# Five matmuls of the identity ahead of the third unit's sums of values

## The chip, the core and the metric

The kernel runs on one core of a Trainium2 chip. The metric is the device time of one execution in microseconds (us). Before the change it is 379.29 us, the median of three runs.

## What is computed

Chunked attention with a left and right context and eight memory keys, followed by a gated MLP with a product over the sequence:

```python
# attention: B, H, S, D = 4, 8, 768, 64; chunks of 32, context 16 left and 8 right, 8 memory rows
scores = scale * np.matmul(q_c, k_full.transpose(0, 1, 3, 2))
scores = scores - np.max(scores, axis=-1, keepdims=True)
a = np.exp(scores)
a = a / (np.sum(a, axis=-1, keepdims=True) + 1e-09)
out[:, :, c_start:c_end] = np.matmul(a, v_full)
# MLP: x is the attention's output, (4, 768, 512); d_ff = 1024
h = np.maximum(x @ w_in, 0.0)
u, v = (h[..., :d_ff // 2], h[..., d_ff // 2:])
v_n = (v - mu) / np.sqrt(var + 1e-06)          # mean and variance over the last axis
v_s = np.einsum('ts,bsd->btd', w_spatial, v_n) + b_spatial[None, :, None]
return ((u * v_s) @ w_out).astype(np.float32)
```

## The kernel before

Attention goes by units of four chunks (128 tokens of one batch, all eight heads); there are 24 units, counted from 0. For unit i a step of the loop over `attend` does the following. ScalarE copies the keys into a padded tile (`kmain`, line 394). TensorE (PE) runs a burst of 64 matmuls of 64 columns that make the scores of unit i (`"s"`), and a burst of 64 that make the sums of values of unit i - 1 (`"a"`); both write the one PSUM tile `sx`, in `burst`, and all of them are recorded at line 409. VectorE takes the maximum (line 466), subtracts it (line 470), ScalarE exponentiates (line 475), VectorE sums and inverts (lines 480 to 483) and multiplies the finished sums of values (line 449). PE transposes the probabilities of unit i (`pt`, line 497) and the finished result of unit i - 1 (`xt`, line 513), and ScalarE and VectorE copy them out of PSUM (lines 500, 518, 522). For units 1 to 5 the two bursts are separate steps of the plan, `"a"` and `"s"`; later they are one.

Between these steps PE runs the first product of the MLP in groups of three matmuls for each quarter of the inner dimension (lines 551 to 553, tile `f`), as soon as the parts of `w_in` and the transposed result are there; ScalarE applies the relu (lines 575 and 612). After the attention come the product over the sequence and the last product (line 700).

The order of all instructions on all engines is written out by `Plan`: each step has an engine, an estimated time, the tiles that it reads and writes, and a rank, and `order` puts the steps in the order of a small simulation. Where this simulation leaves PE idle between 9 and 36 us, `order` puts in spare matmuls of the identity (`busy`, line 249: the 128 x 128 identity as weights, two copies of it as 256 columns to stream, into a PSUM tile `idle` that nothing reads). Loads and stores go through SyncE's queue (SP) in that same order, and `held_by` makes a transfer wait until an earlier one has landed. The values of unit i are loaded by `load_v` in four transfers (into `vmain`); the first matmul of an `"a"` burst waits for these, for the copied probabilities and for the memory rows of the values.

In `burst`, `what` is `"a"` or `"s"` for these units; the step whose `i` is 3 and whose `what` is `"a"` makes the sums of values of unit 2, the third unit.

Of the kernel before, what the change touches and what calls it, by code (L numbers as in the profile page):

```python
# [25 lines left out]
class Plan:  # L26
# [14 lines left out]
    def op(self, eng, us, fn, r=(), w=(), rank=0.0, mb=0.0, tail=0.0, after=None, alone=False, drag=1.0, shared=False):  # L41
        n = len(self.ops)
        deps, begun = set(), set()
        if after is not None:
            begun.add(after)
        for key in r:
            deps.add(self.writer.get(key))
            self.readers.setdefault(key, []).append(n)
        for key in w:
            deps.add(self.writer.get(key))  # L50
            deps.update(self.readers.get(key, ()))
            self.writer[key], self.readers[key] = n, []
        deps -= {None, n}
        held = {k[:2] for k in (*r, *w) if isinstance(k, tuple) and k[0] in self.rings}
        for s in held:
            if s not in self.slots and s[0] not in self.loose:
                if s[0] in self.newest:
                    begun.add(self.newest[s[0]])
                self.newest[s[0]] = n
            self.slots.setdefault(s, []).append(n)  # L60
        begun -= deps
        self.ops.append((eng, us, fn, deps, rank, mb, tail, held, begun, alone, drag, shared))
        return n
# [92 lines left out]
def tile_chunked_attention_gmlp(  # L156
# [47 lines left out]
    op = plan.op  # L204
# [4 lines left out]
    def dve(n):  # L209
        return 0.17 + 0.00102 * n  # L210
# [35 lines left out]
    def busy(k):  # L246

        for _ in range(k):
            nc.tensor.matmul(idle, ident, ident.unsqueeze(1).broadcast_to([P, 2, P]), start=True, stop=True)
# [22 lines left out]
    def wait_for(ins, names, why):  # L272
        for name in names:
            tc.add_manual_dep(ins.ins, name, mybir.DependencyInfo(mybir.DependencyClass.Sync, mybir.DependencyReason.DATA),
                              reason=why)
# [23 lines left out]
    def alloc(name, i, shape, dtype, psum=False):  # L299
        pools = ps if psum else sb  # L300
        a = pools[name].tile(shape, dtype, tag=name, name=name)
        t_[name, i] = a
        return a
# [31 lines left out]
    def qk_keys(i, names="qk"):  # L335
        g, both = i // 2, [0, 1] if i == 1 else [0]
        return [(n, g) + (u, *p) for n in names for u in both for p in ((), ("pad",))]

    def q_of(i):
        return t_["q", i // 2][:, :, (i % 2) * UT:(i % 2) * UT + UT]  # L340
# [4 lines left out]
    def v_of(i):  # L345
        o = (i % NV) * UC
        return vmain[:, :, o:o + UC]
# [24 lines left out]
    def v_keys(i):  # L372
        return [("vm", i, r, s) for r in range(2) for s in range(4)] + \
            [("vmem", i % NV, r) for r in range(2)]
# [29 lines left out]
    def burst(i, rank, split=False):  # L404

        first = []

        def mm(o, w_, m):
            ins = nc.tensor.matmul(o, w_, m, start=True, stop=True, skip_group_check=True)  # L409
            if first:  # L410
                wait_for(ins, first.pop(), "values")

        def go(what):
            if ("sx", i) not in t_:
                alloc("sx", i, [P, 2, 2, T, D], F32, psum=True)
            sx = t_["sx", i]
            if "a" in what:
                first.append([*made["pT", i - 1], *made["v", i - 1], *made["vmem", (i - 1) % NV][-2:]])
            tiles = [(t, c, r, slice(r * D, (r + 1) * D)) for t in range(T) for c in range(UC) for r in range(2)]
            if "s" in what:  # L420
                tq = q_of(i)
                kT = kmain[i % NK].rearrange("p t c s -> p t (c s)")
                for t, c, r, rows in tiles:
                    mm(sx[c * CH:(c + 1) * CH, r, 0, t], tq[rows, t, c * CH:(c + 1) * CH],
                       kT[rows, t, c * SLOT:c * SLOT + WIN])
            if "a" in what:
                pT, vt = t_["pT", i - 1], v_of(i - 1)
                for t, c, r, rows in tiles:
                    mm(sx[c * CH:(c + 1) * CH, r, 1, t], pT[rows, t, c * CH:(c + 1) * CH], vt[rows, t, c])
        whole = ("a" if i >= 1 else "") + ("s" if i < NU else "")  # L430
        for what in (whole if split else [whole]):
            reads, writes = [], []
            us = 0.35
            if "s" in what:
                reads += qk_keys(i, "q") + [("kmain", i % NK), ("kmem", i % NK)]
                writes.append(("sx", i, 0))
                us += 0.5
            if "a" in what:
                reads += [("pT", i - 1)] + v_keys(i - 1)
                writes.append(("sx", i, 1))  # L440
                us += 0.75 if "s" in what else 0.5
            op("PE", us, lambda what=what: go(what), r=reads, w=writes, rank=rank, tail=0.25)
        if i >= 1:
            j = i - 1

            def norm():
                xs = alloc("xs", j, [P, T, 2, D], F32)
                rec = t_["rec", j]
                nc.vector.tensor_tensor(xs.rearrange("p t r d -> p r t d"), t_["sx", i][:, :, 1],  # L449
                                        rec.rearrange("p t r -> p r t").unsqueeze(3).broadcast_to([P, 2, T, D]),  # L450
                                        op=ALU.mult)
            op("DVE", dve(512), norm, r=[("sx", i, 1), ("rec", j)], w=[("xs", j)], rank=rank - 0.5)
        if i < NU:
            softmax(i, rank)

    def softmax(i, rank):
        c0 = (i % UB) * UC

        def top():
            s = t_["sx", i][:, :, 0]  # L460
            if c0 == 0:
                nc.vector.memset(s[0:CH, :, :, 0:LEFT], NEG)
            if c0 + UC == NC:
                nc.vector.memset(s[P - CH:P, :, :, WIN - M:WIN], NEG)
            mx = t_["mx", i] = small.tile([P, 2, T], F32, tag="mx", name="mx")
            nc.vector.tensor_reduce(mx, s, axis=AX.X, op=ALU.max)

        def sub():
            p = alloc("p", i, [P, T, 2, WIN], F32)
            nc.vector.tensor_tensor(p.rearrange("p t r w -> p r t w"), t_["sx", i][:, :, 0],  # L470
                                    t_["mx", i].unsqueeze(3).broadcast_to([P, 2, T, WIN]), op=ALU.subtract)

        def exp():
            p3 = t_["p", i].rearrange("p t r w -> p (t r w)")
            nc.scalar.activation(p3, p3, AF.Exp, scale=scale)

        def den():
            p3 = t_["p", i].rearrange("p t r w -> p (t r) w")
            d = small.tile([P, T * 2], F32, tag="den", name="den")
            nc.vector.tensor_reduce(d, p3, axis=AX.X, op=ALU.add)  # L480
            nc.vector.tensor_tensor(d, d, eps[:, 0:2 * T], op=ALU.add)
            rec = t_["rec", i] = small.tile([P, T, 2], F32, tag="rec", name="rec")
            nc.vector.reciprocal(rec.rearrange("p t r -> p (t r)"), d)

        op("DVE", dve(512) + (0.17 if c0 in (0, NC - UC) else 0), top, r=[("sx", i, 0)],
           w=[("sx", i, 0), ("mx", i)], rank=rank)
        op("DVE", dve(512), sub, r=[("sx", i, 0), ("mx", i)], w=[("p", i)], rank=rank)
        op("ACT", act(512), exp, w=[("p", i)], rank=rank)
        op("DVE", dve(512) + 0.43, den, r=[("p", i)], w=[("rec", i)], rank=rank + 0.6, shared=True)
# [39 lines left out]
    def attend(i, rank, split=False):  # L529
        if i < NU:  # L530
            prep(i, rank)
        burst(i, rank, split)
        flip(i, rank)
# [468 lines left out]
    for b in range(B + 1):  # L1002
        if b < B:
            rank = 300.0 + 10 * b
# [67 lines left out]
```

## Time and profile before

| | |
|---|---|
| median of 3 runs | 379.29 us (375.91 to 380.45) |
| span of the profiled execution | 379.2 us |
| TensorE busy | 357.9 us, 94% |
| VectorE busy | 286.1 us, 75% |
| ScalarE busy | 188.1 us, 50% |
| GpSimd busy | 159.7 us, 42% |

Engines: PE is TensorE's matmuls, PEld its weight loads, DVE VectorE, ACT ScalarE, POOL GpSimd, SP SyncE. Times in the rows are counted from the span's start. A busy share is a mean over stages with different limits; what a change in one stage is worth shows in that stage. In a timeline the bracket at a row's end is the idle time of the engine ahead of it and what ended it; "issue" means that nothing the profile shows ended it. Matmuls are pipelined, so the distance between two starts says more than the time of one. PEclk is TensorE's granted clock: 1.00 is 2.4 GHz, 0.50 is 1.2 GHz.

### The profile page before, as it was taken

To read this page: it belongs to the slowest core of one execution; us is meant where nothing else is said; L and a number is where in the kernel's file an instruction comes from. 1 tells how busy PE (TensorE), PEld (TensorE's weight loads), DVE (VectorE), ACT (ScalarE), POOL (GpSimd) and SP (SyncE) were. 2 spreads that over 40 slices of the span, in tenths; PEclk is the share of its full clock that TensorE was granted. 3 is DMA by queue.
4 is the path that set the end of the run, shared out by engine and by line. 5 is a ranking of instruction groups with operands and counts; after the bars stand their busy time and mean duration, and the time that the engine had idled before them with its cause. 6 is when DMAs were issued, how large, how long until landed. Compare 5 with 4: busy or idle time off the path is not lost.

```text
span 379.2 us, 11840 instructions
## 1 busy us (share of the span) xinstructions
PE 357.9 (94%) x4988; PEld 328.0 (86%) x4988; DVE 286.1 (75%) x479; ACT 188.1 (50%) x334; POOL 159.7 (42%) x155
## 2 busy tenths in 40 slices
PE   2988999999989989989999999999999999999995
PEld 2766787898968968969889898999999999999995
DVE  3878875857747657747389489999979996898893
ACT  3756544555635445434473356346533742653271
POOL 6434562383574086411023275863155124207410
PEclk9998999999999999999999999999999999999999
DMA  8999998788775873876553638404730572140015
GB/s 232 275 194 217 229 271 224 207 257 250 226 218 145 275 214 90 281 206 209 165 206 119 201 124 285 162 3 129 248 124 3 163 246 91 55 155 2 0 45 164
DMA packets 47556, 65.51 MB, mean 173 GB/s; under 512 B 4496, under 2 KB 38928, under 8 KB 47504
## 3 DMA queue, kind: packets, MB, share of 16 engines
q1 hardware_dynamic: 46848, 64.44, 57.3%
q8 instruction: 39, 0.64, 0.7%
q10 hardware_dynamic: 656, 0.33, 0.3%
q14 instruction: 13, 0.11, 0.1%
HBM read 45.88 MB, written 18.87 MB: 171 GB/s over the span
## 4 chain that ended last, share of the span: by engine, by line
PE 82%; DMA 7%; DVE 5%; issue 2%; ACT 1%; SPq 1%; ACTq 0%; DVEq 0%
PE y L700 21%; PE f L700 14%; PE f L551 12%; PE f L552 11%; PE f L553 11%; PE sx L409 8%; DMA vmain<-in_v_dram 6%; PE xt L513 3%; PE pt L497 3%; DVE op L680 2%; DMA big<-in_moe_w_in_dram 2%; DVE sm L663 1%; SPq L278 1%; DVE wout L887 1%; ACT op L677 0%
## 5 line engine op out<-in xcount | busy, mean ns | idle before, releaser
L700 PE MATMUL y<-wsp,op 128*128 128x384 f32 x288 | 52.0, 336 | 0.9 <-ACT st L740 0.9
L754 POOL TENSOR_TENSOR ug<-st,ug 128x384 f32<-128x384 f32 x24 | 36.0, 1515 | 38.5 <-DVE st L746 34.5
L700 PEld LDWEIGHTS y<-wsp,op 128*128 128x128 f32 x288 | 49.9, 188 | 1.2 <-ACT st L740 1.2
L551 PE MATMUL f<-x,win_h 128*128 128x384 f32 x128 | 46.3, 362 | 0.0
L552 PE MATMUL f<-x,win_l 128*128 128x384 f32 x128 | 43.2, 338 | 0.0
L553 PE MATMUL f<-x,win_h 128*128 128x384 f32 x128 | 43.2, 337 | 0.0
L551 PE MATMUL f<-win_h,x 128*128 128x512 f32 x96 | 41.2, 429 | 0.0
L552 PE MATMUL f<-win_h,x 128*128 128x512 f32 x96 | 38.3, 399 | 1.2 <-issue 1.2
L700 PE MATMUL f<-wsp,op 128*128 128x384 f32 x216 | 39.4, 336 | 0.0
L553 PE MATMUL f<-win_l,x 128*128 128x512 f32 x96 | 38.1, 397 | 0.0
L700 PEld LDWEIGHTS f<-wsp,op 128*128 128x128 f32 x216 | 37.6, 188 | 0.0
L680 DVE TENSOR_TENSOR op<-sm,op 128x768 fp32r<-128x768 f32 x32 | 34.8, 1094 | 3.1 <-ACT op L677 2.6
L449 DVE TENSOR_TENSOR xs<-sx,rec 128x512 f32<-128x512 f32 x24 | 16.5, 687 | 27.0 <-PE sx L409 26.9
L587 POOL TENSOR_TENSOR rstd<-ve,mhalf 128x1 f32<-128x1 f32 x24 | 14.6, 608 | 52.0 <-DVE ve L583 49.7
L700 PE MATMUL y<-wout,op 128*128 128x256 f32 x288 | 36.0, 281 | 0.4 <-DVE op L680 0.4
L700 PEld LDWEIGHTS y<-wout,op 128*128 128x128 f32 x288 | 34.8, 188 | 0.9 <-DVE op L680 0.8
L760 POOL TENSOR_TENSOR st<-st,bias 128x384 f32<-128x384 f32 x14 | 18.6, 1337 | 37.2 <-ACT st L740 28.4
L677 ACT CAST op<-sm 128x768 fp32r<-128x768 f32 x32 | 26.2, 837 | 11.6 <-DVE sm L663 10.2
L409 PEld LDWEIGHTS sx<-kmain,q 64*32 64x32 f32 x1536 | 17.0, 107 | 13.9 <-issue 12.0
L388 POOL COPY vmain<-memv 8x1024 f32<-8x1024 f32 x22 | 23.5, 1073 | 11.9 <-PE sx L409 9.8
L409 PE MATMUL sx<-vmain,pT 64*32 64x64 f32 x1536 | 21.9, 226 | 6.1 <-DMA vmain<-in_v_dram 4.1
L409 PE MATMUL sx<-kmain,q 64*32 64x64 f32 x1536 | 20.9, 228 | 6.9 <-ACT kmain L394 6.9
(86 smaller groups left out, 766.3 us busy)
## 6 DMA issues: line engine op xcount, KB each, us to landing
vmain<-in_v_dram SPq DMA_DIRECT2D x48, 128.0 KB
vn_far<-st SPq DMA_DIRECT2D x24, 256.0 KB
u_far<-uo SPq DMA_DIRECT2D x32, 192.0 KB
vr<-vn_far SPq DMA_DIRECT2D x8, 768.0 KB
ug<-u_far SPq DMA_DIRECT2D x16, 384.0 KB
q<-in_q_dram SPq DMA_DIRECT2D x11, 512.0 KB
vmain<-in_v_dram SPq DMA_DIRECT2D x47, 96.0 KB
out_dram<-ot SPq DMA_DIRECT2D x33, 128.0 KB
```

What stands on the lines that cost most here:

```text
L388: ins = {"DVE": nc.vector, "POOL": nc.gpsimd}[eng].tensor_copy(to, of)
L409: ins = nc.tensor.matmul(o, w_, m, start=True, stop=True, skip_group_check=True)
L449: nc.vector.tensor_tensor(xs.rearrange("p t r d -> p r t d"), t_["sx", i][:, :, 1], rec.rearrange("p t r -> p r t").unsqueeze(3).broadcast ...
L551: nc.tensor.matmul(o, lh, rh, start=(j == 0), stop=False)
L552: nc.tensor.matmul(o, ll, rh, start=False, stop=False)
L553: nc.tensor.matmul(o, lh, rl, start=False, stop=(j == len(pairs) - 1))
L587: nc.gpsimd.tensor_tensor(a, t_["ve", i], mhalf, op=ALU.pow)
L677: nc.scalar.copy(half(0), of())
L680: nc.vector.tensor_tensor(half(1), of(), half(0).bitcast(F32), op=ALU.subtract)
L700: nc.tensor.matmul(o, x, y, start=first and m == 1, stop=m == 3 * chunks, skip_group_check=True)
L754: nc.gpsimd.tensor_tensor(g, t_[st(x)], g, op=ALU.mult)
L760: {"DVE": nc.vector, "POOL": nc.gpsimd}[eng].tensor_tensor(a, a, bias[:, 1], op=ALU.add)
```

## The change

The step that makes the third unit's sums of values first calls `busy(5)`: five pairs of weight load and matmul of the identity stand on PE directly in front of the burst's first matmul. The step's estimated time, its reads, writes and rank stay as they were.

```diff
@@ -439,7 +439,11 @@
                 reads += [("pT", i - 1)] + v_keys(i - 1)
                 writes.append(("sx", i, 1))
                 us += 0.75 if "s" in what else 0.5
-            op("PE", us, lambda what=what: go(what), r=reads, w=writes, rank=rank, tail=0.25)
+            def start(what=what):
+                if i == 3 and what == "a":
+                    busy(5)
+                go(what)
+            op("PE", us, start, r=reads, w=writes, rank=rank, tail=0.25)
         if i >= 1:
             j = i - 1
```

## Rows read from the trace of the kernel before

**Rows 1.** The page, engines: busy time, share of the span, instructions.
```profile
PE 357.9 (94%) x4988; PEld 328.0 (86%) x4988; DVE 286.1 (75%) x479; ACT 188.1 (50%) x334; POOL 159.7 (42%) x155
```

**Rows 2.** The chain of waits, 0 to 34 us: start, length, what.
```profile
25.86 7.26 DMA vmain<-in_v_dram
33.12 0.24 issue
```

**Rows 3.** Timeline of PE, 8 to 44 us: start, length, instruction, idle time before.
```profile
8.02 2.67 PE L249 MATMUL idle<-ident 128*128 128x256 f32 x6
...
11.90 5.78 PE L249 MATMUL idle<-ident 128*128 128x256 f32 x26
...
28.23 0.85 PE L409 MATMUL sx<-vmain,pT 64*32 64x64 f32 x64 [1.22 <-DMA vmain<-in_v_dram]
...
29.50 0.60 PE L249 MATMUL idle<-ident 128*128 128x256 f32 x2
...
30.88 0.66 PE L513 MATMUL xt<-ident,xs 128*128 128x128 f32 x4
33.36 0.93 PE L409 MATMUL sx<-vmain,pT 64*32 64x64 f32 x64 [1.83 <-DMA vmain<-in_v_dram]
34.22 0.79 PE L551 MATMUL f<-win_h,x 128*128 128x512 f32 x1
...
36.95 0.92 PE L513 MATMUL xt<-ident,xs 128*128 128x128 f32 x4
37.63 0.48 PE L551 MATMUL f<-win_h,x 128*128 128x512 f32 x1
...
40.47 0.66 PE L497 MATMUL pt<-ident,p 128*128 128x128 f32 x4 [0.36 <-ACT p L475]
40.88 0.48 PE L551 MATMUL f<-win_h,x 128*128 128x512 f32 x1
...
42.45 0.86 PE L409 MATMUL sx<-vmain,pT 64*32 64x64 f32 x64
43.24 0.50 PE L551 MATMUL f<-win_h,x 128*128 128x512 f32 x1
```

**Rows 4.** Stretches: length, each engine's busy time (instructions), PEclk, DMA share, GB/s.
```profile
28.00:31.54 3.54, 3.31 (x138) 2.52 (x138) 2.55 (x7) 2.25 (x5) 2.10 (x3) 1.00 1.04 170
31.54:33.36 1.82, 0.00 (x0) 0.03 (x1) 1.45 (x3) 1.34 (x3) 0.33 (x2) 1.00 0.86 268
34.22:36.95 2.73, 2.73 (x13) 2.04 (x8) 2.56 (x5) 2.07 (x4) 1.00 (x2) 0.50 0.92 194
```

**Rows 5.** Timeline of ScalarE, 37 to 41 us.
```profile
37.91 0.59 ACT L518 CAST x<-xt 128x512 fp32r<-128x512 f32 x1
39.30 0.60 ACT L575 ACTIVATE st<-f 128x512 f32<-128x512 f32 x1 [0.80 <-PE f L553]
39.80 0.62 ACT L475 ACTIVATE p<-p 128x512 f32<-128x512 f32 x1
```

**Rows 6.** Timeline of VectorE, 38 us.
```profile
38.05 0.68 DVE L470 TENSOR_TENSOR p<-sx,mx 128x512 f32<-128x512 f32 x1
```

**Rows 7.** Waits of PE, 30 to 379 us: total, times, longest.
```profile
PE sx L409 <- issue: 1.9, 2, 1.7
PE xt L513 <- issue: 1.7, 1, 1.7
PE f L552 <- issue: 1.2, 1, 1.2
```

**Rows 8.** Stretches between those waits (columns as in rows 4).
```profile
108.80:139.20 30.40, 28.65 (x632) 24.89 (x632) 18.46 (x40) 16.25 (x28) 12.74 (x14) 1.00 0.69 203
139.20:167.70 28.50, 26.80 (x507) 23.13 (x506) 19.18 (x40) 12.72 (x22) 15.19 (x18) 1.00 0.65 190
```

**Rows 9.** The page, DMA queues: packets, MB, share of 16 engines.
```profile
q8 instruction: 39, 0.64, 0.7%
```

**Rows 10.** Timeline of PE, 138 to 141 us.
```profile
138.27 0.79 PE L409 MATMUL sx<-vmain,pT 64*32 64x64 f32 x58
140.80 0.30 PE L409 MATMUL sx<-vmain,pT 64*32 64x64 f32 x4 [1.74 <-issue]
```

## The prediction

> **What bounds the kernel now.** I read the page first, then the chain of waits up to 34 us, the timeline of TensorE (PE) around the changed place, the granted clock by stretches, the queues that feed the next wait (ScalarE and VectorE), and last the waits of PE over the rest of the run.
>
> The page says that PE is the bound as a whole: busy for 357.9 of 379.2 us [rows 1]. So time that is taken off PE's stream shortens the run, if no other engine or transfer takes it back behind the place. The first 33 us are another stage: there the chain of waits ends in a transfer of values, issued at 25.86 and landed 7.26 us later, at 33.12 [rows 2]. That is the transfer of unit 2's values (units count from 0, so this is the third), and the changed burst waits for it.
>
> The timeline [rows 3] shows the place. The transposes of unit 1's result end near 31.54 (30.88 + 0.66). PE then stands for 1.83 us until the burst of unit 2's values begins at 33.36; the row names the transfer. The six f matmuls behind it (lines 551 to 553, twice) start at 34.22, and the next transposes only at 36.95. The clock says why they are slow: 1.00 in the idle stretch and before it, 0.50 from 34.22 to 36.95 [rows 4], which is 1.2 instead of 2.4 GHz. An earlier wait of 1.22 us ends at 28.23 with the clock at 1.00 in the 3.5 us behind it [rows 3, 4]; there PE came from a dense row of f matmuls, and two matmuls of the identity follow at 29.50. Before the longer wait PE had run only a burst and four transposes.
>
> **The change part by part.**
>
> *Added work.* Five pairs of weight load and 256-column matmul. The price is in the timeline: 26 of them took 5.78 us, 0.222 us each; the first six took 2.67 us, 0.445 each [rows 3]. Five cost 1.1 us at the faster pace and 2.2 at the slower. The clock at 31.54 is 1.00 [rows 4], so I take 1.1: they run from 31.54 to about 32.65, in the 1.83 us in which PE stands. What hides them is that wait for the transfer. They themselves wait for nothing, since they read the identity and write a tile that nobody reads. If the transfer came at 31.5, the cover would be gone and they would cost 1.1 us there; at the slower pace they would push the burst by 0.4 (2.2 less 1.83). Behind them on PE stands the burst; for the burst waits VectorE's multiplication that makes unit 2's result, and for that the next transposes. There is no edit of any other queue: no DMA is issued, moved or given a new wait, and the planner's cost of the step is unchanged, so the order of all other instructions stays.
>
> *What they should remove.* The idle stretch becomes about 0.7 us. The stretch that has the low clock, priced against the same work later at the fast clock [rows 3]: the burst takes 33.36 to 34.22, 0.86, against 42.45 to 43.24, 0.79: 0.07. The six f matmuls take 34.22 to 36.95, 2.73, against six from 40.88 to 42.45, 1.57: 1.16. Four transposes take 36.95 to 37.63, 0.68, against 40.47 to 40.88, 0.41: 0.27. Together 1.5 us. Bounds: 0, if the clock falls all the same, and 1.5, if none of the stretch is slow. With the change, PE would run five matmuls of the identity and stand for 0.7 us ahead of the place where the clock fell; around the earlier wait it stood for 1.22 us, ran two of them, and the clock held to 31.54 [rows 3, 4]. The place is nearer to that row than to the one of the fall, so I take 1.5.
>
> *Where the stall goes.* The next wait of PE is at 40.47: the transposes of unit 3's probabilities wait 0.36 us for ScalarE's exponential [rows 3]. If PE arrives 1.5 us sooner and the exponential doesn't move, nothing is left, since the exponential sets 40.47 and the wait only grows. What moves it? ScalarE runs in order: the copy of line 518 at 37.91, the relu of line 575 at 39.30 (it waits 0.80 us for the f group of PE), the exponential of line 475 at 39.80, and one follows another after 0.50 us [rows 5]. The relu's input comes 1.5 us sooner, so the relu can start behind the copy, at about 37.91 + 0.49 = 38.40, and the exponential at 38.90. Its own input, VectorE's subtraction, is ready at 38.05 + 0.68 = 38.73 [rows 6], and that chain does not hang on the slow stretch. So the exponential comes 0.90 us sooner, and the transposes start near 39.57: 0.9 of the 1.5 us stay, and 0.6 become a longer wait there (about 1.0 us instead of 0.36). Bounds of this term: 0 and 1.5; I take 0.9.
>
> *Ten more instructions in PE's stream.* This part has nothing to do with the clock. Three long waits of PE later in the run have no releaser: 1.7, 1.7 and 1.2 us [rows 7]. Between the second and third of the places where they occur (108.8, 139.2, 167.7) lie 632 and 507 pairs [rows 8], that is 1264 and 1014 instructions, close to 5 x 256 and 4 x 256 if some uncounted waits are added. The page has 39 instruction packets of 0.64 MB in all, 16 KB each [rows 9], and twice 4988 instructions [rows 1] over 39 give 256. I read these waits as PE standing at the edge of a block of its own code. Ten more instructions move every later edge to a place five pairs earlier in the work. At 139 us PE has done 58 matmuls of the values when it stops, four short of the burst's end [rows 10]; it would stop about 0.1 us earlier, while the edge before it, 256 instructions back, moves by five of the 0.2 us matmuls ahead of the burst, about 1.1 us. If the fetch starts when that edge is crossed, the wait of 1.74 shrinks by about 1 us. At the other two edges both ends lie among f matmuls and move alike. Bounds for the whole term: three waits gone, -4.6 us, or one new one like the longest, +1.7 us. I take half of the 1 us: -0.5.
>
> The Trainium skill (Runtime: NRT & Kernel Launch, section Instruction fetch mechanics) says that code comes in 16 KiB blocks of 256 instructions and that crossing a block is mostly hidden. The block size agrees with the row's 39 packets; by "hidden" this term would be 0 and the time 378.3, and the three waits speak against that.
>
> *Sum.* 379.2 - 0.9 - 0.5 = 377.8 us. The profiled span of 379.2 is practically the median of the runs, 379.29.
>
> **The rivals.**
>
> 1. *Nothing is gained on the way to the end.* Either the exponential, or something behind it, holds PE at the old time: for it speaks that PE already waits there, for a chain that VectorE feeds; against it that VectorE's subtraction is done 1.1 us before the exponential starts (38.73 and 39.80) [rows 5, 6]. 379.2 less at most the block term: 378.7 to 379.2.
>
> 2. *The clock is not kept, or was not lost in most executions.* Five matmuls may be too few; then the slow stretch stays, and the time is 379.2, or 379.6 if they too run slow. The Trainium skill (TensorE: Matmul & The Clock Gate, Part 1) says that the number of slow matmuls varies between runs of one kernel; by that the median could lack the stretch already, and the time would be 379.2. The one execution here can't show it.
>
> 3. *Slower: the code's edges fall worse.* The place is a burst of 128 pairs, which uses up a whole block in about 1.5 us. An edge that moves to just ahead of a burst turns a fetch that is hidden now into a wait of 1.2 to 1.7 us [rows 7]. It decides from the first new wait on that is longer than the 0.9 us gained: with one of 1.7, 379.2 - 0.9 + 1.7 = 380.0; with two, 381.7. For it: the units all consist of such bursts, with edges at changing places. Against it: ten is little of 256, and the waits that exist are moved too.
>
> **How the numbers follow.** The forecast (clock kept, part of the gain kept) has 0.50, rival 1 has 0.17, rival 2 0.13, rival 3 0.17, and 0.03 is for what I haven't seen. The likeliest gives 377.8, with a range of its own from 376.0 to 378.8 (all of 1.5 and one whole wait of 1.7 gone; or half of 0.9 and no block term). The range of 8 in 10 takes in rivals 1 and 2 and rival 3 with one new wait. Its low end is 1.5 and half of the 4.6, 375.4; its high end is one new wait with nothing gained, 379.2 + 1.7, 381.0. The three runs shown, 375.91 to 380.45, are about as far apart, so the sum's decimals are within what one run differs from another. A measurement of this kernel tells about 2%, 7.6 us, from no change. Faster by that would need more than the whole slow stretch and all the block waits (1.5 + 4.6 = 6.1): 0.02. Slower by that would need five new waits of 1.7: 0.02. Within 2%: 0.96.
>
> **What would show it.** The timeline after should have five matmuls of the identity between the transposes at 30.9 and the burst at 33.4, a wait of some 0.7 us for the same transfer, a granted clock of 1.00 from 34 to 38, six f matmuls in about 1.5 us, and a wait of about 1.0 us at the transposes of unit 3's probabilities. A clock of 0.50 there proves rival 2; that wait grown by the whole 1.5 us proves rival 1; waits without releaser at new places, with more than 4.6 us in sum, prove rival 3. The prediction is wrong if the burst starts later than 33.4 with no wait ahead of it, or if the gain is still growing behind 60 us at places without such waits.

## Result and the profile after the change

The changed kernel is slower. Its median is 382.61 us of 6 runs, that of the kernel before, timed beside it, 377.34 us; the ratio is 1.0104, 95% interval 1.0054 to 1.0153. Timed once more, on another occasion, the ratio was 1.0074 (1.0019 to 1.0128; 381.27 against 376.83 us). The medians here and below are of all runs, the ratios of those that lie no more than 1.5% above the fastest of their kernel. By the ratios the change costs about 0.7 to 1%, 3 to 4 us. The forecast was 377.8 us, a gain of 1.4 on the 379.2 that it started from.

One thing about the scale: the profiled execution of after has a span of 381.2 us and a time of 382.89 us, so about 1.7 us lie around the span. The execution of before that the prediction was made from (span 379.2) was thus among the longer ones, not a median one: with more runs, the medians of before are between 375.6 and 377.3 us.

First the page of after: engines, and the packets that bring instructions.

```profile
PE 360.9 (95%) x4998; PEld 330.6 (87%) x4998; DVE 285.4 (75%) x479; ACT 188.1 (49%) x334; POOL 158.9 (42%) x155
...
q8 instruction: 39, 0.64, 0.8%
```

Five matmuls of the identity are ten records, 4988 to 4998 [rows 1]: in this type the program's one matmul is two pairs of weight load and matmul. It is the same in the bursts: their 64 records are 32 matmuls of the program, not 64. From here on, matmuls and pairs are counted as the profile has them, by records. The waits of PE from 30 us on in after (total, times, longest), which answer to [rows 7]:

```profile
PE sx L409 <- issue: 6.0, 4, 2.4
PE y L704 <- ACT st L744: 0.9, 1, 0.9
PE f L556 <- issue: 0.7, 1, 0.7
PE f L556 <- DVE x L526: 0.5, 1, 0.5
PE y L704 <- DVE op L684: 0.4, 1, 0.4
```

Waits without a releaser are 6.7 us in place of 4.8, and the transfer of values is gone from the list. The timeline of PE in after, which answers to [rows 3]:

```profile
30.30 0.66 PE L517 MATMUL xt<-ident,xs 128*128 128x128 f32 x4
30.79 2.32 PE L249 MATMUL idle<-ident 128*128 128x256 f32 x10
33.04 0.30 PE L409 MATMUL sx<-vmain,pT 64*32 64x64 f32 x3
34.47 0.83 PE L409 MATMUL sx<-vmain,pT 64*32 64x64 f32 x61 [1.13 <-issue]
35.23 0.50 PE L555 MATMUL f<-win_h,x 128*128 128x512 f32 x1
...
36.72 0.60 PE L517 MATMUL xt<-ident,xs 128*128 128x128 f32 x4
...
39.99 0.60 PE L501 MATMUL pt<-ident,p 128*128 128x128 f32 x4
...
51.78 0.80 PE L409 MATMUL sx<-vmain,pT 64*32 64x64 f32 x58
54.24 0.31 PE L409 MATMUL sx<-vmain,pT 64*32 64x64 f32 x6 [1.67 <-issue]
...
107.57 0.79 PE L409 MATMUL sx<-vmain,pT 64*32 64x64 f32 x59
110.78 0.30 PE L409 MATMUL sx<-vmain,pT 64*32 64x64 f32 x3 [2.42 <-issue]
111.00 0.44 PE L555 MATMUL f<-x,win_h 128*128 128x384 f32 x1
```

The ten pairs run from 30.79 to 33.04. The burst begins, does three matmuls, and stops for 1.13 us without a releaser. The f matmuls behind it are fast (35.23 to 36.72, 1.49 us), so the clock was kept there, and at 39.99 the transposes of unit 3 start 0.48 us sooner than at 40.47 before. Then the loss comes, at two places that have nothing to do with the added matmuls: 1.67 us in the burst at 51.8, and 2.42 us in the one at 107.6, near which before stood for 1.69. The burst at 51.8 ran through before:

```profile
52.30 0.85 PE L409 MATMUL sx<-vmain,pT 64*32 64x64 f32 x64
```

Stretches of after, columns as in [rows 4]: the place of the old slow clock, the wait at 108 us, and what follows it.

```profile
34.22:38.00 3.78, 3.53 (x75) 3.00 (x75) 2.60 (x5) 1.12 (x2) 0.76 (x1) 1.00 0.33 85
108.36:110.78 2.42, 0.01 (x2) 0.00 (x1) 0.00 (x0) 0.68 (x1) 2.42 (x2) 1.00 0.62 198
111.60:115.00 3.40, 3.40 (x12) 2.75 (x11) 2.14 (x5) 1.50 (x3) 1.32 (x2) 0.50 0.49 147
```

The clock is 1.00 where it had been 0.50, and 0.50 behind the longer wait at 108 us: the slow stretch wasn't removed, it moved. In the stretch of the wait at 108 us PE does nothing; the DMA queues between 108.2 and 110.8 us hold one packet of instructions among the data:

```profile
q1 hardware_dynamic: 470, 0.53, 63.9%
q8 instruction: 1, 0.02, 2.5%
```

That packet is under way from 108.32 to 109.38, and PE goes on at 110.78, 1.40 us after it landed. This is the rule in all thirteen profiles of this document, of before, of the change and of the experiments below. Behind 30 us they have 45 waits of PE of 0.28 us or more with no releaser, and each ends 1.2 to 1.7 us after a packet of q8 has landed. Counted from PE's first instruction, with weight loads, matmuls and semaphore instructions, each stands at the same place of a period of 256, within one instruction: in after behind 959, 1728, 4031, 5311 and 6336 instructions. So these waits are PE waiting for a block of its own code.

### The profile page after: what moved, and what is told of

Same layout as the page of the kernel before. It is cut to its first block, busy times and chain, and to the rows that moved or that the text cites. A ratio compares the mean times of both kernels' runs of the same rounds, so it can differ in the third digit from the quotient of the medians.

```text
span 381.2 us, 11860 instructions
## 1 busy us (share of the span) xinstructions
PE 360.9 (95%) x4998; PEld 330.6 (87%) x4998; DVE 285.4 (75%) x479; ACT 188.1 (49%) x334; POOL 158.9 (42%) x155
## 4 chain that ended last, share of the span: by engine, by line
PE 84%; DVE 9%; issue 3%; ACT 2%; DMA 1%; SPq 0%; ACTq 0%; DVEq 0%
PE y L704 21%; PE f L704 14%; PE f L555 12%; PE f L556 11%; PE f L557 11%; PE sx L409 9%; PE xt L517 3%; PE pt L501 3%; DVE op L684 2%; DVE sm L667 1%; PE idle L249 1%; DMA k<-in_k_dram 1%; DVE st L868 1%; DVE wout L891 1%; DVE st L867 1%
## 5 line engine op out<-in xcount | busy, mean ns | idle before, releaser
L616 ACT ACTIVATE uo<-f 128x384 f32<-128x384 f32 x32 | 15.6, 492 | 25.9 <-PE f L557 23.8
```

Of the source, the lines that this page charges most:

```text
L616: op("ACT", act(HT), lambda: nc.scalar.activation(alloc("uo", i, [P, HT], F32), t_["f", n], AF.Relu), r=[("f", n)], w=[("uo", i)], rank=rank)
```

## Experiments

Two theories. **A, the edges**: the change adds 20 instructions, so each edge of a 256-instruction block of PE's code falls 20 instructions (ten pairs) earlier in the work; where two edges now come closer in time than a block takes to arrive, PE waits. **B, the time**: the 2.3 us of matmuls in front of the burst delay it, and the delay goes on to the end.

### The instructions without the time (tiny5)

```diff
+    def tiny(k):
+        for _ in range(k):
+            nc.tensor.matmul(idle[0:1, 0, 0:1], mhalf, mhalf, start=True, stop=True)
...
-                    busy(5)
+                    tiny(5)
```

> In place of the five 256-column matmuls of the identity stand five matmuls with one weight column and one streamed column, at the same place: the 20 instructions that the change adds, with hardly any PE time. Theory A (the edges of PE's 256-instruction code blocks moved against the bursts): slower than before by about as much as the change, 2 to 5 us, with waits without releaser near 52.6 and 108 us as after the change. Theory B (the 2.2 us of PE time in front of the burst delay it, and the edges don't matter): as before, within 1 us, with the waits where they were before (108.7, 139.1, 167.6 us).

Measured: 380.19 us median against 376.48; ratio 1.0102 (1.0059 to 1.0145), the same loss as the change. The ten tiny pairs take 0.3 us, and two of its waits stand where the change has them (timeline of PE):

```profile
30.57 0.39 PE L255 MATMUL idle<-mhalf 128*1 128x1 f32 x10
30.89 0.30 PE L414 MATMUL sx<-vmain,pT 64*32 64x64 f32 x3
32.69 0.49 PE L414 MATMUL sx<-vmain,pT 64*32 64x64 f32 x34 [1.50 <-issue]
...
49.98 0.80 PE L414 MATMUL sx<-vmain,pT 64*32 64x64 f32 x58
52.75 0.31 PE L414 MATMUL sx<-vmain,pT 64*32 64x64 f32 x6 [1.97 <-issue]
```

The burst stops behind 3 matmuls and the one at 50 us behind 58, as in after. Near 108 us, where a long wait was expected too, there is only one of 0.3 us; others stand near 137 us (1.1) and 163 us (1.8), at edges where before waits too. B falls as the cause of the loss: without its time the loss is there.

### The time without the shift (back)

```diff
-        for _ in range(k):
-            nc.tensor.matmul(idle, ident, ident.unsqueeze(1).broadcast_to([P, 2, P]), start=True, stop=True)
+        for w in [4] * 5 + [2] * 3 if k == 13 else [2] * k:
+            nc.tensor.matmul(idle[:, 0:w], ident, ident.unsqueeze(1).broadcast_to([P, w, P]), start=True, stop=True)
```

(on the changed kernel; the tile `idle` is widened to four blocks of columns)

> The change, but 10 of the 13 spare matmuls of the identity near 12 to 18 us are put together in pairs to 5 of 512 columns: the same PE time, 20 instructions fewer, so that behind the changed burst every code block ends where it did before the change. Theory A: as before or up to 1.5 us faster, with the waits without releaser of before (about 1.7 us near 108 and 139, 1.2 near 168) and none near 52.6 us. Theory B: slower than before by as much as the change, 2 to 5 us.

Measured: 377.63 us against 376.48; ratio 1.0025 (0.9991 to 1.0058). A loss like the change's is not there, though the interval leaves room for one of 0.6%; the hoped-for gain isn't there either. Its profiled execution was its longest of twelve (380.6 us) and has waits of 1.4 us at 52.3 and 2.5 us at 83.2 us, at edges that didn't move, and that the first profile of before crosses with 0.2 us at most. None was expected near 52 us; so a single profile does not give a kernel's median, and this verdict rests on the ratio.

### Other shifts (start200, start256)

On the kernel before, with `tiny` defined as in tiny5; start256 has `tiny(64)` in this place:

```diff
+        tiny(50)
         plan.emit()
```

> The kernel before, with 50 matmuls of one column (200 instructions) ahead of the first burst, where PE stands idle to 6.9 us: every block edge falls 200 instructions earlier in the work. Theory A: slower than before by 2 to 6 us (a sum over the edges, with 4 to 5 us from one edge to the next block's arrival, gives 4), with the waits at other places than before. Theory B: as before, within 1 us.

> The kernel before, with 64 matmuls of one column (256 instructions, one whole block) ahead of the first burst. Theory A: the edges fall where they did, so as before, within 1 us, with the waits near 108.7, 139 and 168 us. Theory B: as before as well; together with the 200 instructions it tells whether it is the place of the edges or the mere number of instructions.

Measured: 200 instructions ahead of everything, in PE's idle time, 381.76 us, ratio 1.0108 (1.0048 to 1.0169); 256 instructions, 376.89 us, ratio 1.0004 (0.9968 to 1.0041), both against 376.48. More instructions in the second, and no loss: what counts is the number modulo 256, the place of the edges. In the profile of start200 the third unit's burst waits 0.2 us, and the long wait is 2.5 us, at 168 us, in the f matmuls; that execution was one of its quicker ones (span 376.4), so it is not the median's account. In start256 the third unit's burst stops where before's does, as the next experiment shows.

### More profiles of both kernels (after2, after3, before2, before3)

No edit of the kernel.

> The change as it is, once more. Theory A (block edges): slower than before by 0.5 to 1.5%, and a second profile in which the long waits without releaser stand at the same places of the work as in the first (in the values' bursts near 33 and 52.6 us, behind the bursts near 108 and 168 us), with other lengths, since each depends on when its fetch gets through. Theory C (the first profile's waits were chance): the waits stand elsewhere.

> The kernel before against itself. Both theories: the same time within 0.5%. Its profile shows how far the waits without releaser (4.8 us in the first profile) differ between executions: theory A expects them at the same edges (behind the bursts near 108 and 167 us, in the one near 139 us), with other lengths, and a sum below that of the change's profiles (6.7 and 6.0 us).

> The kernel before, one more profile: theory A as for the last one, with a sum of waits without releaser of 2 to 5 us. If the sum is 6 us or more, the waits don't carry the difference between the kernels.

> The change, one more profile: theory A expects a sum of waits without releaser of 5.5 to 7.5 us, with long ones at the edges near 52 and 108 us.

Measured: after2 gave the second ratio above. Before against itself: 375.63 against 376.31 us, ratio 0.9981 (0.9940 to 1.0022). The sums of waits without releaser from 30 us on: before 4.8, 3.1 and 3.0 us, after 6.7, 6.0 and 9.3 us; the means are 3.6 and 7.3, 3.7 us apart, about the loss that the runs show. That is three profiles a side, and after3's 9.3 is above the 5.5 to 7.5 that were expected. Sums of single profiles follow the execution as much as the kernel: tiny5 6.7, back 6.0, start256 6.1 (a longer execution, 379.13 us), two 2.5, and start200, a slower kernel, 3.2. The loss itself rests on the ratios. The waits stand at a few edges in either kernel: in after 1.67, 0.3 and 1.86 us in the burst near 52 us, 2.42, 2.16 and 2.01 near 108; in two of three also 2.57 and 2.31 in the one near 82 us, where before shows at most 0.2 but back, with the edges of before, has 2.5. Not every expected edge waited: near 139 and 167 us, before2 and before3 have at most 0.2 where the first profile has 1.74 and 1.16, and after2 has none near 33 and 0.3 near 52. The waits of PE from 30 us on, in before3 and then in after3:

```profile
PE sx L409 <- issue: 1.8, 2, 1.6
PE xt L513 <- issue: 1.2, 1, 1.2
```

```profile
PE sx L409 <- issue: 7.0, 4, 2.3
PE f L556 <- issue: 2.3, 1, 2.3
```

They also correct the picture of the changed place. The timeline of PE there, before3, then start256:

```profile
30.15 0.66 PE L513 MATMUL xt<-ident,xs 128*128 128x128 f32 x4
30.74 0.33 PE L409 MATMUL sx<-vmain,pT 64*32 64x64 f32 x13
32.64 0.74 PE L409 MATMUL sx<-vmain,pT 64*32 64x64 f32 x51 [1.57 <-issue]
```

```profile
30.52 0.33 PE L414 MATMUL sx<-vmain,pT 64*32 64x64 f32 x13
33.29 0.74 PE L414 MATMUL sx<-vmain,pT 64*32 64x64 f32 x51 [2.43 <-issue]
```

Here the transfer has landed in time: the burst starts right behind the transposes and stops after 13 matmuls for 1.57 and 2.43 us, with no releaser. Three matmuls in after and tiny5, 13 in before3 and start256: ten pairs apart, the 20 instructions. So in these two executions it is a block of code that holds the burst, not the values. In before2 the burst first waits 0.77 us, by the profile for ScalarE's copy of line 518, and then stops after 13 matmuls for 1.21. The timeline of after2 at the place:

```profile
30.49 2.32 PE L249 MATMUL idle<-ident 128*128 128x256 f32 x10
32.74 0.86 PE L409 MATMUL sx<-vmain,pT 64*32 64x64 f32 x64
```

The identity matmuls run while the block would have been waited for, and the burst goes on at 32.74 against 32.64 in before3. At the place itself the change neither costs nor gains much.

### Fewer matmuls at the place (two)

Against the kernel of back:

```diff
-        for w in [4] * 5 + [2] * 3 if k == 13 else [2] * k:
+        for w in [4] * 2 + [2] * 9 if k == 13 else [2] * k:
...
-                    busy(5)
+                    busy(2)
```

> Two matmuls of the identity (0.9 us) in place of five (2.2 us) ahead of the burst, and four spare matmuls near 12 to 18 us put together in pairs, so that no block edge behind the burst moves. Theory A with a smaller delay of the burst: the clock falls in fewer executions than before, the burst is held up by at most 0.9 us, and the time is that of before or up to 1.5 us less. Theory B: 1 to 2 us slower than before.

Measured: 376.19 against 376.31 us, ratio 1.0014 (0.9975 to 1.0052): as before. The clock: of the 66 executions of before that were timed beside the experiments, 42 have a mean granted clock of 0.997 or more (median 375.9 us, the other 24: 378.7); of 24 of back and two, 21; of 17 of the change, only 7 (median 378.9 us, the other ten 383.1). So the added matmuls, if no edge moves, seem to hold the clock more often; that is not proven, since nine of the ten executions of before2 hold it too. Kernels with moved edges lose it more often: of 15 executions of tiny5 and start200, 3 hold it. In the three profiles of the change the slow stretch stands behind one of the longer waits, at 108, 108 and 82 us. And even the change's executions with the clock held are 3 us longer than before's.

### The bursts apart (split, split5)

On the kernel before (split) and on the changed one (split5):

```diff
-        attend(i, 10.0 * i, 1 <= i < UB)
+        attend(i, 10.0 * i, 1 <= i)
```

> The kernel before, with the two bursts of every unit as separate steps of the plan (as units 1 to 5 have them), so that f matmuls mostly stand between them: 256 instructions of PE then hold some f matmuls wherever they start. Theory A: the waits without releaser in the attention shrink from 4.8 us to under 2 us, and the time falls by 1 to 4 us unless the other order costs something. Theory B: no fewer waits.

> The same with the change's five matmuls. Theory A: with the bursts apart, 20 instructions more or less no longer matter, so the time is that of the separated bursts without the five matmuls, within 1.5 us. Theory B: 2 to 5 us slower than that.

Measured: 382.55 us, ratio 1.0148 (1.0089 to 1.0207), and with the change 383.80 us, ratio 1.0175 (1.0116 to 1.0235), against 376.83. The first expectation failed: the plan puts every engine's work in another order with the bursts apart, and the sum of waits without releaser from 40 us on is 3.3 us, where less than 2 was expected, and more than in the later profiles of before (1.9 and 1.4; 4.8 in the first). The second came out as A has it, 1.25 us between the two, but the intervals are too wide for that to be proof. I did not pursue where the other order loses.

## Why the prediction was wrong

**Added work: mis-sized.** The step priced five pairs from a row whose count is of records, not of the program's matmuls [rows 3]. It is ten pairs, 2.3 us instead of 1.1 (30.79 to 33.04), and 20 instructions instead of ten. That they would lie in the time in which PE stands held: 32.74 against 32.64 us at the burst.

**The wait's cause: right for one execution only.** The profile of before has the transfer landing at 33.12 [rows 2]. In before3 the values are there, and in before2 and before3 the burst stops inside, at an edge of the code. In the first profile the packet for this edge landed at 32.27 us; with the 1.2 to 1.7 us of the other waits, code would have held the burst to 33.5 or later there too (an estimate). The rows of one execution were taken for the kernel.

**The clock: the mechanism held, its weight didn't.** The clock was kept at 34 to 38 us in all three profiles of the change (granted clock 1.00), as forecast. But before loses it, at this place or another, in about a third of its executions only (24 of 66), so little of the 0.9 us could show in a median; that was the second half of rival 2. The Trainium skill (TensorE: Matmul & The Clock Gate, Part 1) says that the number of slow matmuls varies between runs of one kernel. It says so of a kernel's start; here it varies in the middle as well. With the edges put back, the change was 1.0025 (0.9991 to 1.0058), no measurable gain.

**The next wait: in part.** The transposes of unit 3 did come sooner, by 0.48 us in the first profile; the forecast of 0.9 had the burst start at 33.4, and it started at 33.04, stopped, and went on at 34.47.

**The block term: the step that failed.** The prediction had the mechanism (PE waits at the edges of 256-instruction blocks, and the change moves them) and put it at -0.5 us. The waits measured about +3.7 us, from 3.6 to 7.3 in the mean of three profiles each. Two faults. It priced only the edges that already had a wait in the profile, and not those that had just none: the one near 52 us lay ten pairs beyond its new place, in f matmuls with 0.2 us from one to the next, and moved into the last six matmuls of a burst, where the distance to the edge ahead of it shrank from 3.9 to 3.1 us by the place in the order of instructions (49.87 to 53.72 before, 49.26 to 52.36 in after). The shorter distance is 0.8 of the 1.67 us; most of the rest is the packet, which landed 3.6 us behind the edge ahead of it in after (at 52.84) and 2.5 behind it in before (at 52.38). In after2 it landed 2.1 us behind, and the wait is 0.3.

And it took the wait at 108 us as unchanged, since both ends "lie among f matmuls". They did not: the edge ahead stood 0.1 us inside a burst (105.78, the burst begins at 105.70), and the later one among transposes, as the timeline of PE in before shows:

```profile
108.45 0.27 PE L513 MATMUL xt<-ident,xs 128*128 128x128 f32 x1
110.41 0.49 PE L513 MATMUL xt<-ident,xs 128*128 128x128 f32 x3 [1.69 <-issue]
```

In after the edges lie ten pairs earlier: PE stops behind 59 of the burst's matmuls, 1.9 us behind the edge ahead (106.47 to 108.36) and not 2.9 (105.78 to 108.72), and the wait went from 1.69 to 2.42 us. At 139 us the direction was right, as the timeline of after shows, but in before's other profiles there was hardly a wait to shrink:

```profile
143.38 0.34 PE L409 MATMUL sx<-vmain,pT 64*32 64x64 f32 x14 [0.81 <-issue]
```

Rival 3 named the mechanism, with a chance of 0.17 and a price of one new wait; two or three new or longer ones are what came, near its 381.7 us, and by the prediction's own sign (waits without releaser at new places, more than 4.6 us in sum) it is what happened.

The sentence of the Trainium skill that crossing a block is mostly hidden (Runtime: NRT & Kernel Launch, Instruction fetch mechanics) holds for most of the 39 packets. It does not hold for all: one to five of them in a profile leave waits of 0.28 us or more, up to 2.6 us.

**The range** (375.4 to 381.0) ended at one new wait with nothing gained; 382.61 lies outside. That the sum was made on 379.2, where the medians of before with more runs are 375.6 to 377.3, hid a part of the error: against the kernel before, 1.4 us were to be gained, and 3 to 4 were lost.

What stays open: why the long waits near 82 us come in some executions and not in others. They stand at an edge in a burst. The packet itself took 1.0 to 1.4 us at this edge with the wait and without it; what differs is its start, 4.1 and 3.8 us behind the edge ahead in after2 and after3, 1.0 in after, at most 0.4 in the profiles of before. The queues are busy there; that the fetch has to get through behind other packets is argued, not shown.

## What to carry to other kernels

Added instructions are not free where the engine stands idle: they shift all code behind them, and a kernel with dense bursts of tiny instructions can lose more at the edges of its code blocks than the edit was to gain. Before judging such an edit, time it once with its instructions taken out elsewhere, or with tiny ones in its place, so that work and shift are told apart. Look at waits without a releaser in several profiles, count the records up to them, and price the edges that just miss a wait too.

## What the runs showed of the hardware

PE's code comes in blocks of 256 instructions (39 packets, 0.64 MB), and PE went on 1.2 to 1.7 us after the packet that it waited for had landed. A burst of 128 pairs of 64 x 32 weights uses one block up in about 1.5 us; at an edge inside or behind such a burst PE stood for up to 2.6 us. The effect is periodic: 20 or 200 instructions more cost 1%, 256 more cost nothing (1.0004). A plain matmul of 32-bit floats is two pairs of records (ten for the five of the identity); a transpose is one. And a wait of 2.42 us for code, like one of 1.83 us for data, was followed by a stretch at half the clock; waits of 2.57 us in after2 and 2.54 in back, both near 83 us, were not.
